# Attention and gated feed-forward on one core: the late heads' softmax weights transposed by VectorE and DMAs, their value products in float32 in two column streams

## The chip, the core and the metric

The program runs on one NeuronCore of a Trainium2 chip. The metric is the device time of one execution in microseconds (us); less is better. A core has a matrix engine (TensorE, called PE in the profile, its weight loads PEld), VectorE (DVE), ScalarE (ACT), GpSimd (POOL) and SyncE (SP), which here only issues DMAs. The engines run side by side, each through its own list of instructions in order, and wait for one another at semaphores.

## What is computed

Causal block attention for 8 batches and 8 heads (576 positions, head size 64, blocks of 64), and a feed-forward layer behind it, with 4608 tokens, width 512 and inner width 2048:

```python
scores = scale * np.matmul(q, k.transpose(0, 1, 3, 2))
mask = block_i >= block_j                       # blocks of 64 positions
scores = np.where(mask, scores, -1000000000.0)
scores = scores - np.max(scores, axis=-1, keepdims=True)
attn = np.exp(scores)
attn = attn / (np.sum(attn, axis=-1, keepdims=True) + 1e-09)
x = np.matmul(attn, v)                          # then heads side by side: 4608 x 512
h = x @ w_in
g = h * (1.0 / (1.0 + np.exp(-1.702 * h)))
out = g @ w_out
```

q, k and v are float32, and the two weight matrices arrive as float64.

## The kernel before, in words

**Two strands on one matrix engine.** The 64 heads are taken one after the other (loop at L568, one step a head). The feed-forward layer is a generator, `moe()` (L475), that is advanced between the parts of a head by `advance` (L543) until a quota of work for that point of the loop (`TILES_BY`, L35) is reached. It works on 12 tiles of 384 tokens. For each tile it goes over 16 chunks of the inner width; a chunk is 12 matmuls into the tile `hp` (L507) and, one chunk later, 9 matmuls into the three tiles `acc` (L479). In the steps of the late heads three chunks lie in a step, in six half portions: 36 matmuls `hp` and 27 matmuls `acc`. All matmuls keep the order in which the program writes them (`mm`, L92, and `tr`, L95).

**Chunks of queries.** The 576 queries of a head are cut into five chunks, i = 0 to 4, of 64, 128, 128, 128 and 128 rows; chunk i looks at 64 x (2i+1) keys. A step of the loop computes the scores of head n (`score`, L291, six parts S0 to S5; S4 and S5 are the two halves of chunk 4), and the value product of head n-1.

**What a score part does.** Two matmuls write the scores into a PSUM bank; DVE adds the mask, scales, and takes the row's extreme value (L313, into the tile `e` of the chunk); ACT takes the exponential and the row sum (L321); DVE turns the sums into reciprocals (L330, L333); the chunk is multiplied by them (L340 to L344, on the engine that `SCALE_ON` names).

**Early and late heads.** The first 17 heads (`EARLY`) and the other 47 differ. A late head loads q and k in strips (`load`, L194: four DMAs L214, two copies L218), turns them with a DVE transpose of 32x32 blocks (L244, L248) and splits them into a high and a low part (L245 to L250). For the value product the weights must stand with the keys on the partitions. `fill` (L368) does this before the change for all heads: PE transposes 128x128 blocks of `e` against an identity (L95, 15 a head, in four fills F1 to F4), and ACT copies the bank to `ph` (L386, L389). For a late head DVE also writes the rest into `pl` (L390) and mends the diagonal blocks (L396); the values are split in the same way into `vs` (L253, L254), with a copy `vd` made by two DMAs (L257). The value product `av` (L401), in two parts A and B, then is 14 matmuls of the format float32r (high and low parts against both halves of `vs`), and ACT and DVE add the two halves into `xr` (L430, L431). For an early head `av` is plain float32 against `vn`, and one float32 matmul stands in the profile as two records.

**The order of a step** is written out in `ORDER` (L28), one row for each phase; a blank there is where `moe()` is advanced. The late row before is `S0+F2 S1+F3 F4 S2 A S3 S4 F1+S5 B`.

Of the kernel before, what the change touches and what calls it, by code (L numbers as in the profile page):

```python
# [15 lines left out]
PSUM = bass.MemoryType.PSUM  # L16


EARLY = 17


SCALE_ON = ("APPPD", "DDPPP", "DDDDD")

GROUPS = (2, 3, 4)

ORDER = (  # L28
# [3 lines left out]
)  # L32

WEIGHTS_BY = ((0, 0), (9, 30), (15, 64))
TILES_BY = ((8.8, 0), (17, 1), (65, -2))  # L35
# [3 lines left out]
def attention_moe_kernel(  # L39
# [9 lines left out]
    nc = tc.nc  # L49
# [65 lines left out]
    for i in range(NCH):  # L115
# [2 lines left out]
        if i == 0:  # L118
            nc.gpsimd.memset(e[BLK:P, 0:BLK], 0.0)
        es.append(e)  # L120
    vr = sp.tile([P, NCH, D], F32, name="vr")
    nc.gpsimd.memset(vr[BLK:P, NCH - 1, :], 0.0)

    def width(i):
        return BLK * (2 * i + 1)
# [23 lines left out]

    def weight_piece(j, roomy):  # L150
        src, hi, lo = pieces[j]
        m = d2.tile([P, 2, WC], U32, tag=f"pl{1 + j % 2}", name="wm", bufs=1)
        halves = []
        for a in range(2):
            if roomy:
                w = xr[:, 2 * (j % 2) + a : 2 * (j % 2) + a + 1, S : S + 2 * WC].bitcast(U32)
            else:
                w = d2.tile([P, 1, 2 * WC], U32, tag="osb", name="wst", bufs=3)
            d = nc.sync.dma_start(out=w, in_=src[:, a : a + 1])
# [34 lines left out]
    def load(n):  # L194
        b, h = divmod(n, H)
        raw[n] = []
        for src in (q[b, h], k[b, h]):
            if early(n):

                t = d2.tile([P, NCH, 2, D], F32, tag="hl", name="qkr", bufs=3)  # L200
                parts = [
                    (t[:, 0:QC], src[0 : QC * P].rearrange("(p c) d -> p c d", c=QC).unsqueeze(2).to_broadcast([P, QC, 2, D])),
                    (t[0:BLK, QC], src[QC * P : S].unsqueeze(1).to_broadcast([BLK, 2, D])),
                ]
                queue = nc.scalar if n == 0 and len(raw[n]) else nc.sync
                for o, i in parts:
                    d = queue.dma_start(out=o, in_=i)
                    if n < 2:
                        tc.keep_in_program_order(d)
            else:  # L210

                t = d2.tile([P, S // 32, 32], F32, tag="hl", name="qkd", bufs=3)
                for c in range(0, D, 32):
                    nc.sync.dma_start(  # L214
                        out=t[c : c + 32],
                        in_=src[:, c : c + 32].rearrange("(c p) d -> p c d", p=32),
                    )
                nc.sync.dma_start(out=t[D:P], in_=t[0:D])  # L218
            raw[n].append(t)
        if not early(n):  # L220
            load_v(n, vr)

    def load_v(n, t):
        b, h = divmod(n, H)
        nc.sync.dma_start(
            out=t[:, 0:QC, :], in_=v[b, h, 0 : QC * P].rearrange("(c p) d -> p c d", p=P)
        )

        for r in (0,) if early(n) else (0, BLK):
            nc.sync.dma_start(out=t[r : r + BLK, QC, :], in_=v[b, h, QC * P : S])  # L230

    qk, vs, vd = {}, {}, {}

    def prep(n):
        qk1 = d2.tile([P, 2, S], F32R, tag="qk1", name="qk1")
# [12 lines left out]
        nc.vector.transpose(out=tmp, in_=kr.rearrange("p c d -> p (c d)"))  # L248
        nc.scalar.copy(out=k1, in_=tmp)
        subtract(nc.vector, k1[D:P], tmp[D:P], f(k1[D:P]))  # L250

        vs[n] = d2.tile([P, NCH, 2, D], F32R, tag="vs", name="vs")
        nc.scalar.copy(out=vs[n][:, :, 0, :], in_=vr)  # L253
        subtract(nc.vector, vs[n][:, :, 1, :], vr, f(vs[n][:, :, 0, :]))  # L254
        vd[n] = d2.tile([P, 2, D], F32R, tag="vd", name="vd")
        for r in (0, BLK):
            nc.sync.dma_start(out=f(vd[n][r : r + BLK]), in_=f(vs[n][0:BLK, 2]))  # L257

    def turn(n, which):
        qs, ks, qk1, q2 = qk[n]  # L260
# [30 lines left out]
    def score(n, ci):  # L291
# [42 lines left out]
        for ii in range(c0, i + 1):  # L334
# [7 lines left out]
                nc.vector.tensor_scalar(out=x, in0=x, scalar1=sc, scalar2=None, op0=ALU.mult)  # L342
# [10 lines left out]
    DIAG = ((2, 256), (4, 512))  # L353

    def blocks(j, q0, nq):
        res = []
# [11 lines left out]
    def fill(n, fi):  # L368


        pad, parts = FILLS[fi]
        tot = sum(p[2] for p in parts)
        bk = bank()
        tp = bk[:, pad : pad + tot]
        todo = []
        off = pad
        for j, q0, nq in parts:
            todo += [(j, off, *blk) for blk in blocks(j, q0, nq)]
            off += nq
# [3 lines left out]
        hi = d2.tile([P, tot], F32 if early(n) else F32R, tag=f"ph{fi}", name="ph", bufs=1)  # L383
        lo = None
        if early(n):
            nc.scalar.copy(out=hi, in_=tp[:, 0:tot])  # L386
        else:
            lo = d2.tile([P, tot], F32R, tag=f"pl{fi}", name="pl", bufs=1)
            nc.scalar.copy(out=hi, in_=tp[:, 0:tot])  # L389
            nc.vector.tensor_tensor(out=lo, in0=tp[:, 0:tot], in1=f(hi), op=ALU.subtract)  # L390
        off = 0
        for j, q0, nq in parts:
            c = slice(off, off + nq)
            pt[n, j, q0] = (hi[:, c], lo[:, c] if lo is not None else None)
            if not early(n) and (j, q0) in DIAG:
                nc.vector.tensor_tensor(  # L396
                    out=hi[BLK:P, c], in0=tp[BLK:P, c], in1=f(hi[BLK:P, c]), op=ALU.subtract
                )
            off += nq

    def av(n, parts, q0, nq):  # L401
# [2 lines left out]
        o = bank()  # L404
        r = (h % 2) * D
        c0 = (b % 2) * S + q0
        x = xr[r : r + D, h // 2, c0 : c0 + nq]

        todo = []
        for j, qs0, nn in parts:  # L410
            hi, lo = pt.pop((n, j, qs0))
            if early(n):
                kk = P if j < QC else BLK
                todo.append((vs[n][0:kk, j], hi[0:kk], qs0, nn))
            elif (j, qs0) in DIAG:
                vv = vs[n][:, j] if j == QC else vd[n]
                todo.insert(1, (vv.rearrange("p a d -> p (a d)"), hi, qs0, nn))
            else:
                vv = vs[n][:, j].rearrange("p a d -> p (a d)")
                todo[1:1] = [(vv, x, qs0, nn) for x in (hi, lo)]  # L420
        for cnt, (vv, w, qs0, nn) in enumerate(todo):
            mm(
                out=o[0 : vv.shape[1], qs0 - q0 : qs0 - q0 + nn], lhsT=vv, rhs=w,
                start=cnt == 0, stop=cnt == len(todo) - 1,
            )
        if early(n):
            (nc.scalar.copy if q0 else nc.vector.tensor_copy)(out=x, in_=o[0:D, 0:nq])  # L427
        else:

            nc.scalar.copy(out=x, in_=o[D - r : P - r, 0:nq])  # L430
            nc.vector.tensor_tensor(out=x, in0=o[r : r + D, 0:nq], in1=x, op=ALU.add)  # L431


    FILLS = [(0, PA[0:1]), (0, PB[0:1] + PA[1:3]), (0, PB[1:3]), (BLK, PB[3:5])]
# [1 line left out]
    def step(n):  # L436
# [4 lines left out]
        def on(c, fn, *a):  # L441
            return (lambda: fn(*a)) if c else None

        items = dict(
            F2=on(prev, fill, n - 1, 1), F3=on(prev, fill, n - 1, 2), F4=on(prev, fill, n - 1, 3),
            F1=on(now, fill, n, 0), A=on(prev, av, n - 1, PA, 0, SA), B=on(prev, av, n - 1, PB, SA, SB),
            Q=on(trn, turn, n + 1, 0), K=on(trn, turn, n + 1, 1), R=on(trn, turn, n + 1, 2),
        )
        for ci in range(6):
            items[f"S{ci}"] = on(now, score, n, ci)  # L450
        return [[items[y] for y in x.split("+")] for x in ORDER[phase(n)].split()]


    done = {"split": 0}
# [113 lines left out]
    for n in range(NHEAD + 1):  # L568
        if n + 1 < NHEAD:
            prep(n + 1)  # L570
        if n + 2 < NHEAD and not early(n + 1):
            load(n + 2)
        if n < NHEAD and early(n):
            vs[n] = d2.tile([P, NCH, D], F32, tag="vs", name="vn")
            load_v(n, vs[n])
        items = step(n)
        for sl, it in enumerate(items):
            for fn in it:
# [39 lines left out]
```

## Time and profile before

| | before |
|---|---|
| median of 3 runs | 1218.6 us (1217.72 to 1220.04) |
| profiled execution, its own time | 1218.16 us |
| its span, first to last instruction | 1216.4 us |
| instructions | 20880 |
| mean granted PE clock | 0.994 |
| DMA traffic | 78.62 MB |

The profile is of one execution. Its page gives each engine's busy time, the span in 40 slices, the chain of work that ended last, and groups of like instructions: line, engine, operation, output and input by the program's names, the count, and then the busy time, the mean of one in ns, and the idle time before them. The views used beside the page are the timeline (start, length, engine, line, with equal neighbours merged as x2, x3), the chain of waits in a window, and all instructions of one line with their shortest, median and longest length. Matmuls overlap: a record's length holds a drain that the next one covers, so that what one costs is the distance to the next start.

### The profile page before, as it was taken

To read this page: it belongs to the slowest core of one execution; us is meant where nothing else is said; L and a number is where in the kernel's file an instruction comes from. 1 tells how busy PE (TensorE), PEld (TensorE's weight loads), DVE (VectorE), ACT (ScalarE), POOL (GpSimd) and SP (SyncE) were. 2 spreads that over 40 slices of the span, in tenths; PEclk is the share of its full clock that TensorE was granted. 3 is DMA by queue.
4 is the path that set the end of the run, shared out by engine and by line. 5 is a ranking of instruction groups with operands and counts; after the bars stand their busy time and mean duration, and the time that the engine had idled before them with its cause. 6 is when DMAs were issued, how large, how long until landed. Compare 5 with 4: busy or idle time off the path is not lost.

```text
span 1216.4 us, 20880 instructions
## 1 busy us (share of the span) xinstructions
PE 1188.4 (98%) x6860; PEld 1063.9 (87%) x6860; DVE 872.0 (72%) x2460; ACT 706.7 (58%) x1773; POOL 367.6 (30%) x496
## 2 busy tenths in 40 slices
PE   6899999999999999999999999999999999999998
PEld 5667887789999999999999999999999999999997
DVE  6997788777887888778888787878788788611111
ACT  6886666655665565656665665565575566432322
POOL 3554454421321312321322232232132231232321
PEclk8999999999999999999999999999999999999999
DMA  8653444422222231232132232222232231000000
GB/s 201 162 152 94 118 117 119 108 42 51 50 70 44 55 76 40 48 81 50 38 76 55 44 70 50 51 70 45 53 76 43 46 77 30 4 26 1 27 1 26
DMA packets 223772, 78.62 MB, mean 65 GB/s; under 512 B 198832, under 2 KB 204848, under 8 KB 223664
## 3 DMA queue, kind: packets, MB, share of 16 engines
q1 hardware_dynamic: 222480, 77.00, 27.0%
q8 instruction: 54, 0.88, 0.3%
q14 instruction: 54, 0.44, 0.1%
q10 hardware_dynamic: 1184, 0.30, 0.1%
HBM read 50.87 MB, written 9.44 MB: 50 GB/s over the span
## 4 chain that ended last, share of the span: by engine, by line
PE 87%; DVE 7%; ACT 2%; issue 2%; DMA 1%; POOL 1%; POOLq 0%; SPq 0%; DVEq 0%; ACTq 0%
PE hp L92 32%; PE acc L92 32%; PE bank L92 15%; PE bank L95 8%; DVE e L313 1%; DVE wm L171 1%; DVE wm L176 1%; ACT e L321 1%; DVE sm L330 1%; DVE wm L167 1%; DVE e L342 1%; DVE qk L286 1%; DMA wst<-in_moe_w_out_dram 0%; DMA qkr<-in_q_dram 0%; DVE xr L427 0%
## 5 line engine op out<-in xcount | busy, mean ns | idle before, releaser
L81 POOL TENSOR_TENSOR gl<-g,gh 128x384 fp32r<-128x384 f32 x192 | 197.2, 1027 | 599.5 <-ACT gh L522 521.7
L321 ACT ACTIVATE e<-e,mx 64x64 f32<-64x64 f32 (+4 forms) x320 | 180.0, 563 | 214.8 <-DVE mx L313 213.8
L92 PE MATMUL hp<-xh,wih 128*128 128x384 f32 x768 | 268.0, 349 | 2.4 <-ACT wih L180 1.9
L92 PE MATMUL hp<-xl,wih 128*128 128x384 f32 x768 | 259.6, 338 | 1.2 <-POOL sm L297 1.2
L92 PE MATMUL hp<-xh,wil 128*128 128x384 f32 x768 | 259.0, 337 | 0.9 <-POOL wil L81 0.9
L92 PE MATMUL acc<-woh,gh 128*128 128x512 f32 x576 | 237.0, 412 | 0.5 <-ACT woh L180 0.5
L92 PE MATMUL acc<-wol,gh 128*128 128x512 f32 x576 | 227.2, 395 | 0.6 <-POOL wol L81 0.6
L92 PE MATMUL acc<-woh,gl 128*128 128x512 f32 x576 | 226.7, 394 | 0.5 <-POOL gl L81 0.5
L518 DVE SCALAR_TENSOR_TENSOR g<-g,hp 128x384 f32<-128x384 f32 x192 | 105.3, 548 | 129.4 <-ACT g L517 128.3
L313 DVE CUSTOM_DVE_ANT_0 e<-bank,mask 64x64 f32<-64x64 f32 (+4 forms) x320 | 132.9, 420 | 69.3 <-PE bank L92 65.6
L517 ACT ACTIVATE g<-hp 128x384 f32<-128x384 f32 x192 | 93.9, 489 | 119.2 <-PE hp L92 115.9
L95 PE MATMUL bank<-ident,e 128*128 128x128 f32 x960 | 153.9, 280 | 8.1 <-DVE e L342 5.6
L92 PEld LDWEIGHTS hp<-xh,wih 128*128 128x128 f32 x768 | 144.6, 188 | 11.5 <-ACT wih L180 2.1
L92 PEld LDWEIGHTS hp<-xh,wil 128*128 128x128 f32 x768 | 144.9, 189 | 9.6 <-POOL wil L81 1.2
L92 PEld LDWEIGHTS hp<-xl,wih 128*128 128x128 f32 x768 | 144.3, 188 | 1.6 <-POOL sm L297 1.6
L390 DVE TENSOR_TENSOR pl<-bank,ph 128x512 fp32r<-128x512 f32 (+2 forms) x188 | 102.4, 562 | 56.7 <-ACT ph L389 56.6
L342 DVE TENSOR_SCALAR e<-e,sm 64x64 f32<-64x64 f32 (+2 forms) x260 | 137.2, 557 | 4.9
L92 PEld LDWEIGHTS acc<-wol,gh 128*128 128x128 f32 x576 | 108.3, 188 | 26.2 <-POOL wol L81 1.1
L95 PEld LDWEIGHTS bank<-ident,e 128*128 128x128 f32 x960 | 112.1, 142 | 21.1 <-DVE e L342 8.0
L522 ACT CAST gh<-g 128x384 fp32r<-128x384 f32 x192 | 97.6, 508 | 52.9 <-DVE g L518 52.2
L92 PE MATMUL bank<-qk 128*128 128x320 f32 (+4 forms) x384 | 118.3, 308 | 2.7 <-DVE qk L286 1.8
L92 PEld LDWEIGHTS acc<-woh,gh 128*128 128x128 f32 x576 | 108.7, 189 | 11.0 <-ACT woh L180 0.7
(68 smaller groups left out, 1845.4 us busy)
## 6 DMA issues: line engine op xcount, KB each, us to landing
qkd<-qkd SPq DMA_DIRECT2D x94, 144.0 KB, 2.3
out_dram<-osb SPq DMA_DIRECT2D x36, 256.0 KB, 2.1
qkd<-in_q_dram SPq DMA_DIRECT2D x94, 72.0 KB, 2.4
qkd<-in_k_dram SPq DMA_DIRECT2D x94, 72.0 KB, 2.2
vr<-in_v_dram SPq DMA_DIRECT2D x47, 128.0 KB, 2.4
wst<-in_moe_w_out_dram SPq DMA_DIRECT2D x18, 256.0 KB, 3.2
qkr<-in_q_dram SPq DMA_DIRECT2D x17, 256.0 KB, 3.4
xr<-in_moe_w_in_dram SPq DMA_DIRECT2D x16, 256.0 KB, 3.1
```

The source lines that it names most:

```text
L81: eng.tensor_tensor(out=out, in0=in0, in1=in1, op=ALU.subtract)
L92: return tc.keep_in_program_order(nc.tensor.matmul(**kw))
L95: return tc.keep_in_program_order(nc.tensor.transpose(**kw))
L167: nc.vector.tensor_scalar(out=m, in0=m, scalar1=3, scalar2=None, op0=ALU.logical_shift_left)
L171: nc.vector.scalar_tensor_tensor(out=y, in0=w[..., 1], scalar=0x80000000, in1=y, op0=ALU.bitwise_and, op1=ALU.bitwise_or,)
L313: nc.vector.tensor_tensor_reduce(out=e[0:m, lo:hi], in0=s[0:m, 0 : hi - lo], in1=mk, op0=ALU.add, op1=ALU.min, scale=-0.125, scalar=3e38 i ...
L321: nc.scalar.activation(out=e[0:m, 0:w], in_=e[0:m, 0:w], func=AF.Exp, scale=-1.0, bias=mx[0:m, i : i + 1], accum_out=sm[0:m, i : i + 1],)
L342: nc.vector.tensor_scalar(out=x, in0=x, scalar1=sc, scalar2=None, op0=ALU.mult)
L390: nc.vector.tensor_tensor(out=lo, in0=tp[:, 0:tot], in1=f(hi), op=ALU.subtract)
L517: nc.scalar.activation(out=g, in_=hp[:, 0:tt], func=AF.Tanh, scale=1.702)
L518: nc.vector.scalar_tensor_tensor(out=g, in0=g, scalar=1.0, in1=hp[:, 0:tt], op0=ALU.add, op1=ALU.mult)
L522: nc.scalar.copy(out=gh, in_=g)
```

## The change

For early heads only buffers change: `fill` copies into slices of one tile `tw`, the values lie in the two tiles `v0` and `v1`, and the weight conversion uses `pw` as its scratch. For a late head:

- `fill`, `av`, the split of the values and the two DMAs of `vd` go. The fills, A and B are gone from the order.
- After a chunk is scaled, DVE transposes its 32x32 blocks into the tile `tw` (L355 of the changed kernel, chunks 1 to 4; L360, the 64x64 diagonal piece of each chunk). This turns each block in place and leaves it on the partitions of its queries.
- When chunk 4 is done, 16 DMAs on SP (L367) carry the blocks of each pair (block of keys, block of queries) to the partitions of their keys, in the tile `pw`. Each moves 32 partitions, one run of 1280 to 1792 bytes on each. There is one tile `tw` and one tile `pw`, used by every late head.
- `av_late`, item V, is 15 float32 matmuls against the unsplit values. Each has 64 columns of weights: those of chunks 4, 1 and 0 write PSUM partitions 0 to 63, those of chunks 3 and 2 partitions 64 to 127, and the two lists are merged by their position. 832 columns are streamed on one side and 768 on the other. ACT copies the result to `xr` in three pieces.
- The late row of the order is `S0+S1 S2 S3 S4 V S5`, and the step between the phases has a row of its own. V of head n-1 thus stands in step n, behind the fourth of six half portions of the feed-forward layer.
- Of a late head's five scalings, chunk 1's goes from DVE to POOL and chunk 3's from DVE to ACT; POOL's copies of L346 go.

```diff
-SCALE_ON = ("APPPD", "DDPPP", "DDDDD")
+SCALE_ON = ("APPPD", "DDPPP", "DPDAD")
...
-    "S0+F2 S1+F3 F4 S2 A S3 S4 F1+S5 B",
+    "S0+S1 S2 S3 S4 V S5",
...
+    NS = 14
+    SLOT = (None, 0, 1, 3, 6)
+    tw = sp.tile([P, 4 * NS * 32], F32, name="tw")
+    pw = sp.tile([P, 4 * NS * 32], F32, name="pw")
+    twv, pwv = [x.rearrange("p (b s c) -> p b s c", b=4, s=NS) for x in (tw, pw)]
...
-            if not early(n) and ii in (2, 4):
-                nc.gpsimd.tensor_copy(out=es[ii][BLK:P, we : we + BLK], in_=es[ii][BLK:P, we - BLK : we])
+            if early(n):
+                continue
+            if ii:
+                nc.vector.transpose(
+                    out=twv[:, :, SLOT[ii] : SLOT[ii] + ii, :].rearrange("p b j c -> p j b c"),
+                    in_=es[ii][:, 0 : ii * P],
+                )
+            r = slice(BLK, P) if ii else slice(0, BLK)
+            nc.vector.transpose(
+                out=twv[r, 0:2, 9 + max(ii, 1), :], in_=es[ii][r, ii * P : ii * P + BLK]
+            )
+        if not early(n) and i == NCH - 1:
+            for kb in range(4):
+                for qb in range(4):
+                    ns = 10 if kb > 1 else 14 if qb > 1 else 11
+                    nc.sync.dma_start(
+                        out=pwv[kb * 32 : kb * 32 + 32, qb, 0:ns, :],
+                        in_=twv[qb * 32 : qb * 32 + 32, kb, 0:ns, :],
+                    )
...
+    SIDES = (((4, 192), (1, 64), (0, 0)), ((3, 128), (2, 0)))
+
+    def av_late(n):
...
+        for side, chunks in zip((0, D), SIDES):
+            for i, c in chunks:
+                t = [(c, P, j, pwv[:, :, SLOT[i] + j, :]) for j in range(i)]
+                a, w = (2, c + BLK) if i else (0, c)
+                t.append((w, BLK, i, pwv[:, a : a + 2, 9 + max(i, 1), :]))
+                for w, nn, j, rhs in t:
+                    todo.append((sum(y[1] for y in todo if y[2] == side), nn, side, w, j, rhs))
+        todo.sort(key=lambda y: y[0])
...
+        for x, (pos, nn, side, w, j, rhs) in enumerate(todo):
+            mm(
+                out=o[side : side + D, w : w + nn].rearrange("d (a c) -> d a c", c=32),
+                lhsT=v2[n % 2][:, j], rhs=rhs, start=pos == 0, stop=x == ends[side],
+            )
```

SP's list before, one late head: `qkd` are strips of q and k, `vr` the values, `vd` the copy of a piece of the split values.

```order
L218 DMA qkd<-qkd 64x576
L214 DMA qkd<-in_q_dram 32x18x32 x2
L218 DMA qkd<-qkd 64x576
L214 DMA qkd<-in_k_dram 32x18x32 x2
L257 DMA vd<-vs 64x128 x2
L225 DMA vr<-in_v_dram 128x4x64
L230 DMA vr<-in_v_dram 64x64 x2
```

SP's list after, one late head: the 16 DMAs from `tw` to `pw` and then the loads of the next heads.

```order
L367 DMA pw<-tw 32x352 x2
L367 DMA pw<-tw 32x448 x2
L367 DMA pw<-tw 32x352 x2
L367 DMA pw<-tw 32x448 x2
L367 DMA pw<-tw 32x320 x8
L235 DMA qkd<-qkd 64x576
L231 DMA qkd<-in_k_dram 32x18x32 x2
L241 DMA v_90<-in_v_dram 128x4x64
L244 DMA v_90<-in_v_dram 64x64
L231 DMA qkd<-in_q_dram 32x18x32
L235 DMA qkd<-qkd 64x576
L231 DMA qkd<-in_q_dram 32x18x32
```

SP issues 24 DMAs a late head where it issued 11, and the 16 stand in one row without anything between them.

PE's list before, the larger part of a late head's value product (B), between two groups of `hp`:

```order
L92 MATMUL bank<-ph,vs 128x256
L92 MATMUL bank<-ph,vs 128x64
L92 MATMUL bank<-ph,vs 128x192
L92 MATMUL bank<-pl,vs 128x192
L92 MATMUL bank<-ph,vs 128x256
L92 MATMUL bank<-pl,vs 128x256
L92 MATMUL bank<-ph,vs 128x256
L92 MATMUL bank<-pl,vs 128x256 x2
```

PE's list after, the whole value product (V), with the last matmul of the group of `hp` ahead of it and the first of the group of `acc` behind it:

```order
L96 MATMUL hp<-xl,wih 128x384
L96 MATMUL bank<-pw,v_92 64x128 x7
L96 MATMUL bank<-pw,v_92 64x64
L96 MATMUL bank<-pw,v_92 64x128
L96 MATMUL bank<-pw,v_92 64x64
L96 MATMUL bank<-pw,v_92 64x128 x2
L96 MATMUL bank<-pw,v_92 64x64 x3
L96 MATMUL acc_5947<-woh,gh 128x512
```

The rows of `ident,e`, 15 a head before, are gone. The first matmul of V waits for all 16 DMAs of its head.

DVE's list between the two halves of chunk 4 before, with what each row waits for (`e_86` is chunk 3, `e_88` chunk 4):

```order
L313 ISA e_88,mx<-bank,mask 128x256 [waits PE_49]
L313 ISA mx 128x1
L330 TENSOR_SCALAR sm<-sm 128x1 [waits Activation_49]
L518 SCALAR_TENSOR_TENSOR g<-g,hp 128x384 [waits Activation_49]
L333 RECIPROCAL sm<-sm 128x1 [waits DVE_49]
L342 TENSOR_SCALAR e_86<-e_86,sm 128x448 [waits DVE_49]
L313 ISA e_88,mx<-bank,mask,mx 128x320 [waits PE_49]
```

The same place after (`e_82` is chunk 1, `e_84` chunk 2):

```order
L360 STREAM_TRANSPOSE tw<-e_86 64x2x32 [waits Activation_49]
L546 SCALAR_TENSOR_TENSOR g<-g,hp 128x384 [waits Activation_49]
L355 STREAM_TRANSPOSE tw<-e_82 128x4x32 [waits DMAHW4_49,DMAHW5_49,DMAHW3_49,DMAHW6_49,DMAHW2_49,DMAHW7_49,DMAHW1_49,DMAHW0_49]
L355 STREAM_TRANSPOSE tw<-e_84 128x2x4x32
L355 STREAM_TRANSPOSE tw<-e_86 128x3x4x32
L258 STREAM_TRANSPOSE tmp<-qkd 128x576 [waits DMAHW0_49]
L320 ISA e_88,mx<-bank,mask,mx 128x320 [waits DVE_49,PE_49]
```

The transposes of chunks 1 to 3 wait until the DMAs of the head before have read `tw`. Chunk 4's two transposes stand after its scaling and S0's reduction of the next step, and the 16 DMAs wait for them.

More of the change, by code (lines that the diff above doesn't have):

```diff
@@ L227, in load_v @@
         )
-        for r in (0,) if early(n) else (0, BLK):
-            nc.sync.dma_start(out=t[r : r + BLK, QC, :], in_=v[b, h, QC * P : S])
-    qk, vs, vd = {}, {}, {}
+        nc.sync.dma_start(out=t[0:BLK, QC, :], in_=v[b, h, QC * P : S])
+    qk = {}
     def prep(n):
@@ L382, in fill @@
             tr(out=bk[:, c : c + P], in_=es[i][:, j * P : (j + 1) * P], identity=ident)
[L383 to L390, printed above, removed]
+        o = sum(sum(p[2] for p in x[1]) for x in FILLS[:fi])
+        hi = tw[:, o : o + tot]
+        nc.scalar.copy(out=hi, in_=tp)
         off = 0
         for j, q0, nq in parts:
[L393 to L398, printed above, removed]
+            pt[n, j, q0] = hi[:, off : off + nq]
             off += nq
@@ L421, in av @@
-        for cnt, (vv, w, qs0, nn) in enumerate(todo):
-            mm(
-                out=o[0 : vv.shape[1], qs0 - q0 : qs0 - q0 + nn], lhsT=vv, rhs=w,
-                start=cnt == 0, stop=cnt == len(todo) - 1,
-            )
[L426 to L431, printed above, removed]
+        for cnt, (j, qs0, nn) in enumerate(parts):
+            kk = P if j < QC else BLK
+            mm(
+                out=o[0:D, qs0 - q0 : qs0 - q0 + nn], lhsT=v2[n % 2][0:kk, j], rhs=pt.pop((n, j, qs0))[0:kk],
+                start=cnt == 0, stop=cnt == len(parts) - 1,
+            )
@@ L444, in step @@
         items = dict(
+            V=on(prev and not early(n - 1), av_late, n - 1),
             F2=on(prev, fill, n - 1, 1), F3=on(prev, fill, n - 1, 2), F4=on(prev, fill, n - 1, 3),
@@ L572, in attention_moe_kernel @@
             load(n + 2)
[L573 to L575 removed]
+        if n < NHEAD:
+            load_v(n)
+        if n == EARLY:
+            nc.gpsimd.memset(pwv[BLK:P, :, 10:NS, :], 0.0)
         items = step(n)
```

50 lines of the change are left out of this document (24 added, 26 removed).

## The prediction

> **What bounds the kernel now.** I read the page's busy times first, then the chain of waits inside one late head, then one stage by engine.
>
> ```profile
> span 1216.4 us, 20880 instructions
> PE 1188.4 (98%) x6860; PEld 1063.9 (87%) x6860; DVE 872.0 (72%) x2460; ACT 706.7 (58%) x1773; POOL 367.6 (30%) x496
> 400.00:600.00 200.00, 200.00 (x1187) 184.81 (x1185) 161.50 (x443) 118.75 (x297) 49.41 (x76) 1.00 0.26 56
> ```
>
> The last row is a window in the middle of the late heads: PE has no idle time, DVE is busy 161.50 of 200 us, ACT 118.75, and the granted clock is 1.00. In the chain of waits between 400 and 418 us every piece is PE's own (start, length, tile and line, records):
>
> ```profile
> by line: PE hp L92 38.0%; PE acc L92 34.6%; PE bank L92 17.8%; PE bank L95 11.2%
> ...
> 400.18 0.33 PE bank L95 x3
> ...
> 401.86 1.39 PE acc L92 x6
> 403.25 0.63 PE bank L92 x5
> 403.88 0.69 PE acc L92 x3
> ...
> 408.73 0.33 PE bank L95 x3
> 409.06 0.30 PE bank L92 x2
> ...
> 411.13 1.06 PE bank L92 x9
> ...
> 413.33 0.60 PE bank L95 x5
> ...
> 415.51 0.44 PE bank L95 x4
> ...
> 417.71 0.33 PE bank L95 x3
> ```
>
> The same fill returns at 417.71, 17.53 us after 400.18: that is the period of a late head, and PE fills it without a gap. So before the change the end is set by the sum of PE's work, and a us taken off PE in each of the 47 late heads is 47 us, as long as nothing else takes PE's place.
>
> **What PE loses and gains.** The fills (L95: 0.33, 0.60, 0.44 and 0.33) are 1.70 us of a period and the two value products (0.63 and 1.06) 1.69 us. Both go: 3.39 us a head, and 14.14 us stay. V is new. Its price is read at the float32 value product of an early head, which has the same 64 columns of weights; the timeline of PE and PEld:
>
> ```profile
> 111.81 0.39 PE L92 MATMUL acc<-woh,gl 128*128 128x512 f32 x1
> 112.05 0.40 PE L92 MATMUL acc<-wol,gh 128*128 128x512 f32 x1
> 112.37 0.65 PE L92 MATMUL bank<-ph,vn 128*64 128x256 f32 x2
> 112.37 0.86 PE L92 MATMUL bank<-ph,vn 128*64 128x256 f32 x3
> 112.37 1.49 PEld L92 LDWEIGHTS bank<-ph,vn 128*64 128x64 f32 x8 [0.37 <-issue]
> 114.39 0.50 PE L92 MATMUL acc<-woh,gh 128*128 128x512 f32 x1
> 114.73 0.39 PE L92 MATMUL acc<-woh,gl 128*128 128x512 f32 x1
> ```
>
> Two answers end after two and after three records: a third of 256 columns adds 0.21 us, 0.82 ns a column. A float32 matmul is two such records. V's longer stream, 832 columns, is 2 x 832 x 0.82 ns = 1.37 us if the shorter one runs beside it; both one after the other are 2 x 1600 x 0.82 = 2.62 us. Around it the array changes from 128 to 64 columns: the first record starts 0.32 us behind an `acc` where the `acc` before it took 0.24, and behind the block the first `acc` takes 0.34. That is 0.09 and 0.10 us, and about as much again for the first load and the gap at the end; I count 0.35 us. No trace of before has two streams at once; I take them side by side, because they write different partitions and have different columns of weights. V then is 1.75 us (3.0 in sequence), and PE's own sum is 14.14 + 1.75 = 15.89 us a head.
>
> Side by side is also what the Trainium skill says ("TensorEngine Tiling (Array Packing)", Key Properties: tiles operate independently); no run here shows it yet.
>
> **The new wait.** V waits for its head's 16 DMAs; these wait for DVE's transposes of chunk 4; these for S5. From S5 to V, PE has the rest of its sum to do, 15.89 less V, an `acc` group (0.69 + 1.39 = 2.08) and S5 (0.30): 11.76 us. If DVE, ACT and the DMAs take longer, PE stands at V, and everything in its list behind V stands with it. The chain up to the DMAs, on PE, ACT and DVE, in the present kernel:
>
> ```profile
> 812.35 0.31 PE L92 MATMUL bank<-qk,q 128*128 128x320 f32 x1
> 812.70 0.55 DVE L313 CUSTOM_DVE_ANT_0 e<-bank,mask,mx 128x320 f32<-128x320 f32 x1 [0.23 <-PE bank L92]
> 813.30 0.78 ACT L321 ACTIVATE e<-e,mx 128x576 f32<-128x576 f32 x1
> 814.25 0.15 DVE L330 TENSOR_SCALAR sm<-sm 128x1 f32<-128x1 f32 x1
> 814.38 0.78 DVE L248 STREAM_TRANSPOSE tmp<-qkd 128x576 f32<-128x576 f32 x1
> 815.08 0.12 DVE L333 RECIPROCAL sm<-sm 128x1 f32<-128x1 f32 x1
> 815.24 0.52 DVE L342 TENSOR_SCALAR e<-e,sm 128x576 f32<-128x576 f32 x1
> 817.51 0.20 DVE L313 CUSTOM_DVE_ANT_0 e<-bank,mask 64x64 f32<-64x64 f32 x1
> ```
>
> From S5's second matmul at 812.35 to the end of the scaling at 815.76 are 3.41 us. The transpose between (814.38 to 815.08) stands ahead of S5 in the new list: 2.71 us. Behind the scaling come S0's reduction, 0.20, and the transpose of chunk 4, 512 columns. The nearest row:
>
> ```profile
> L244 DVE STREAM_TRANSPOSE tmp<-qkd 128x576 f32<-128x576 f32 x47 | 36.0, 765 | 0.5 <-DVE sm L330 0.4
> L390 DVE TENSOR_TENSOR pl<-bank,ph 128x512 fp32r<-128x512 f32 (+2 forms) x188 | 102.4, 562 | 56.7 <-ACT ph L389 56.6
> L431 DVE TENSOR_TENSOR xr<-bank,xr 64x320 f32<-64x320 f32 x47 | 22.8, 485 | 2.0 <-ACT xr L430 1.3
> ```
>
> 512/576 of 765 ns are 0.68 us. With 0.05 to reach SP the first DMA starts 2.71 + 0.20 + 0.68 + 0.05 = 3.64 us behind S5's second matmul.
>
> **The 16 DMAs** are the disputed cost. SP's rows, by line (shortest, median, longest in ns) and in the timeline:
>
> ```profile
> L214 SPq DMA_DIRECT2D qkd<-in_k_dram x94: 311/489/1622, 211.6 to 1008.5; - x94
> L257 SPq DMA_DIRECT2D vd<-vs x94: 467/536/772, 220.2 to 1045.0; - x94
> 18.25 0.33 SPq L159 DMA_DIRECT2D xr<-in_moe_w_out_dram  x1
> 18.64 0.42 SPq L159 DMA_DIRECT2D wst<-in_moe_w_out_dram  x1
> 796.80 1.11 SPq L257 DMA_DIRECT2D vd<-vs  x2
> 797.96 0.58 SPq L225 DMA_DIRECT2D vr<-in_v_dram  x1
> 798.58 1.15 SPq L230 DMA_DIRECT2D vr<-in_v_dram  x2
> 799.77 1.12 SPq L214 DMA_DIRECT2D qkd<-in_k_dram  x2
> vd<-vs SPq DMA_DIRECT2D x94, 32.0 KB, 1.8
> qkd<-qkd SPq DMA_DIRECT2D x94, 144.0 KB, 2.3
> ```
>
> A DMA holds SP for 0.3 to 0.6 us, longer when another stands right ahead, and 0.05 us lie between two (18.25 + 0.33 to 18.64). The trains differ: 128 partitions with one run each (L159) 0.42 + 0.05 = 0.47 us a DMA; 32 partitions with 18 runs each (L214) 0.49 + 0.05 = 0.54; 64 partitions (L257, L230) about 0.60 (796.80 to 798.58 are three DMAs, 0.59 each), and up to 0.64. The new DMAs have 32 partitions and one run on each. The only rows with 32 partitions are the cheapest when alone (0.31), and their train carries 18 runs a partition; fewer runs should cost no more, so I take 0.47, between the ends 0.43 and 0.64. Landing: 32 KB take 1.8 us, 144 KB 2.3; for at most 56 KB I take 1.9.
>
> The loop from V to the next V then is V 1.75 + `acc` 2.08 + S5's first matmul 0.15 + 3.64 + 15 x 0.47 = 7.05 + 1.9 = 16.57 us. It is longer than PE's sum, 15.89: PE waits 0.68 us at every V, and a late head takes 16.57 us, not 17.53. In general the loop is 9.52 us + 15 times the distance of two DMAs; it meets PE's sum at 0.425 us and the present period at 0.534 us.
>
> **The other edits.** DVE loses L390 (102.4 / 47 = 2.18 us a head), L431 (its two parts 0.9) and more; it gains 1280 columns of transposes, 1.33 ns each, 1.70 us, and five pieces of 64 columns at about 0.2, as S0's reduction takes. So its share stays near 0.8 and the transposes are hidden, but for chunk 4's 0.68. DVE's transposes of chunks 1 to 3 wait for the same DMAs as V and have V, `acc` and S5 as cover (4.0 us for 1.02 + 0.77 of L258); behind them only S5's reduction is queued. ACT loses four copies and gains three smaller ones and a scaling; POOL swaps two copies for one scaling. SP issues 24 DMAs a head, 11.3 to 14.4 us, inside the period. The early heads' edits cost nothing: same copies, other buffers.
>
> **The sum.** 47 x (17.53 - 16.57) = 45 us. In the last step no scores stand ahead of V and PE waits about 1 us more. The profiled execution took 1218.16 us by its own time, 0.4 below the median of the runs and inside their spread, so no correction is made: 1218.2 - 44 = 1174 us. This likeliest case by itself goes from 1145 (0.43 us a DMA) to 1210 (0.52).
>
> **The rivals.**
> - *The queue becomes the bound* (slower; chance 0.29). At the price of the 64-partition rows, 0.64, the loop is 19.12 us, 1.59 more than now: 1218 + 75 = 1293 us; at 0.59 it is 1258. It decides from 0.534 on. For it: `vd` too goes from SBUF to SBUF with one run a partition. Against it: the 32-partition rows are cheaper. With it PE would stand 2 to 3 us at each V.
> - *The queue is hidden* (faster; 0.08). Below 0.425 PE's sum remains: 47 x 1.64 = 77 us, 1141 us.
> - *The two streams run in sequence* (slower; 0.07). V is 3.0 us; with my price for the DMAs the loop is 17.82: 1232 us.
> - *The loads stand out* (slower; 0.02). The eight loads at 112.37 lie inside their block, so a load goes on beside the running matmul. If alternating sides undid that, each of 30 records would expose half of the 0.10 us that the 128-column load showed: 1.5 us, loop 18.07, 1243 us. The Trainium skill ("TensorE: Matmul & The Clock Gate", Part 3) says that a load overlaps a running matmul only where the row groups differ, and both sides use all rows; the eight loads, all on the same rows, do not agree.
> - *No difference* (0.04): a distance of about 0.53.
>
> **How the numbers follow.** A measurement of this kernel tells about 0.2% from no change, 2.4 us. Faster: 0.50 + 0.08 = 0.58. Same: 0.04. Slower: 0.29 + 0.07 + 0.02 = 0.38. The range reaches from 1140, with the hidden queue, to 1258, a distance of 0.59 us; what lies above, about 0.18, is left out.
>
> **What would show it.** In the new profile: the distance of two L367 rows on SP (0.47); their landing (1.9); PE's idle time ahead of V, by the release of a `pw` DMA (0.7 us, 47 times); the period (16.6); V's 30 records in 1.4 us, in pairs. Wrong would be: V over 2.5 us, a distance above 0.53, or a larger wait that another engine ends, DVE's `g` above all.

## The result and the profile after

The changed kernel takes 1393.59 us (median of 4 runs, 1390.01 to 1402.86), the kernel before 1218.16 us beside it: a ratio of 1.145, 95% interval 1.139 to 1.151. It is 175 us slower; the prediction had 45 us faster, and even its slow rival had 1293.

The page of the changed kernel: the span, the engines' busy shares, the granted clock in 40 slices, and the chain that ended last by engine and by line.

```profile
span 1388.8 us, 21590 instructions
PE 1196.5 (86%) x6907; PEld 1045.0 (75%) x6907; DVE 767.1 (55%) x2366; ACT 647.7 (47%) x1632; POOL 371.4 (27%) x451
...
PEclk9999999998988999899999999998998999899999
...
PE 37%; SPq 25%; DVE 19%; DMA 7%; issue 6%; ACT 5%; POOL 0%; DVEq 0%; POOLq 0%; ACTq 0%
SPq L367 25%; PE acc L96 15%; PE bank L96 13%; PE hp L96 7%; DMA pw<-tw 6%; DVE e L320 3%; ACT e L328 2%; DVE e L349 2%; DVE tw L355 2%; DVE q L85 2%; DVE tmp L262 2%; ACT qk L259 1%; DVE g L546 1%; DVE qk L85 1%; PE bank L99 1%
```

Before, PE was 98% busy and every piece of the chain inside a late head was its own. Now PE is 86% busy, and the largest line of the chain is L367, SP issuing the 16 DMAs. The waits of the late heads say where PE stands (total us, times, longest):

```profile
PE bank L96 <- DMA pw<-tw: 148.6, 47, 5.2
...
DVE tw L355 <- DMA pw<-tw: 90.3, 46, 4.0
...
DVE g L546 <- ACT g L545: 65.9, 47, 3.7
```

47 times, once a head, PE stands 148.6 / 47 = 3.16 us ahead of V for the last DMA. The place is the predicted one, the size is not (0.68 us). One head, V to V, from two windows of the timeline; the rows of DVE show the chain behind S5:

```profile
802.74 2.93 PE L96 MATMUL bank<-pw,v 128*64 128x128 f32 x30 [3.25 <-DMA pw<-tw]
...
805.60 0.50 PE L96 MATMUL acc<-woh,gh 128*128 128x512 f32 x1
...
807.94 0.31 PE L96 MATMUL bank<-qk,q 128*128 128x320 f32 x1
808.28 0.55 DVE L320 CUSTOM_DVE_ANT_0 e<-bank,mask,mx 128x320 f32<-128x320 f32 x1 [3.77 <-PE bank L96]
...
810.34 0.52 DVE L349 TENSOR_SCALAR e<-e,sm 128x576 f32<-128x576 f32 x1
...
810.92 0.70 DVE L355 STREAM_TRANSPOSE tw<-e 128x512 f32<-128x512 f32 x1
...
811.72 10.04 SPq L367 DMA_DIRECT2D pw<-tw  x16
...
823.54 0.66 PE L96 MATMUL bank<-pw,v 128*64 128x128 f32 x8 [2.91 <-DMA pw<-tw]
```

Each start less the one before is a term of the predicted loop. The right column is the mean over the 46 distances from V to V, read in the same way from the trace:

| term | predicted, us | this head | mean of 46 |
|---|---|---|---|
| V | 1.75 | 2.86 | 2.64 |
| `acc` and S5's first matmul | 2.23 | 2.34 | 2.61 |
| S5's second matmul to the first DMA | 3.64 | 3.78 | 4.10 |
| first to last DMA | 7.05 | 9.45 | 9.65 |
| last DMA to V | 1.90 | 2.37 | 2.09 |
| loop | 16.57 | 20.80 | 21.09 |

The 16 DMAs last 10.04 us with 0.59 for the last: (10.04 - 0.59) / 15 = 0.63 us apart. 47 x (21.09 - 17.53) = 167 us of the 175 are this loop; the rest lies ahead of the first of these V's and behind the last.

V itself has two prices (2.5 us and more for 37 of the 47, under 1.8 for 8). Windows of three V's: from and to, their length, busy time (records) of PE, PEld, DVE, ACT and POOL, PE's granted clock, the DMA share and GB/s:

```profile
781.68:784.61 2.93, 2.93 (x30) 2.82 (x30) 1.81 (x4) 0.00 (x0) 0.00 (x0) 0.50 0.72 141
...
802.74:805.60 2.86, 2.86 (x31) 2.79 (x31) 1.77 (x4) 0.00 (x0) 0.00 (x0) 0.53 0.72 140
823.54:825.09 1.55, 1.55 (x30) 1.49 (x30) 1.03 (x3) 0.00 (x0) 0.00 (x0) 1.00 0.36 61
```

The same 30 records take 1.55 us at a clock of 1.00 and 2.93 at 0.50. The `acc` group behind V pays too where the clock stays low: in the slowest heads its term is 3.2 to 3.7 us instead of 2.34. So two things had to be tested: what sets 0.63 us, and whether the wait itself makes V dear.

### The profile page after: what moved, and what is told of

It is laid out like the page before. It is cut to its first block, busy times and chain, and to the rows that moved or that the text cites. A ratio compares the mean times of both kernels' runs of the same rounds, so it can differ in the third digit from the quotient of the medians.

```text
span 1388.8 us, 21590 instructions
## 1 busy us (share of the span) xinstructions
PE 1196.5 (86%) x6907; PEld 1045.0 (75%) x6907; DVE 767.1 (55%) x2366; ACT 647.7 (47%) x1632; POOL 371.4 (27%) x451
## 4 chain that ended last, share of the span: by engine, by line
PE 37%; SPq 25%; DVE 19%; DMA 7%; issue 6%; ACT 5%; POOL 0%; DVEq 0%; POOLq 0%; ACTq 0%
SPq L367 25%; PE acc L96 15%; PE bank L96 13%; PE hp L96 7%; DMA pw<-tw 6%; DVE e L320 3%; ACT e L328 2%; DVE e L349 2%; DVE tw L355 2%; DVE q L85 2%; DVE tmp L262 2%; ACT qk L259 1%; DVE g L546 1%; DVE qk L85 1%; PE bank L99 1%
## 5 line engine op out<-in xcount | busy, mean ns | idle before, releaser
L85 POOL TENSOR_TENSOR gl<-g,gh 128x384 fp32r<-128x384 f32 x192 | 196.6, 1024 | 452.1 <-ACT gh L550 408.2
L96 PE MATMUL bank<-pw,v 128*64 128x128 f32 (+1 forms) x1410 | 127.8, 361 | 148.6 <-DMA pw<-tw 148.6
L96 PE MATMUL acc<-woh,gh 128*128 128x512 f32 x576 | 245.0, 425 | 1.2 <-ACT woh L197 1.2
L96 PEld LDWEIGHTS bank<-pw,v 128*64 128x64 f32 x1410 | 120.8, 207 | 162.4 <-issue 127.6
L96 PE MATMUL acc<-woh,gl 128*128 128x512 f32 x576 | 233.2, 405 | 0.5 <-POOL gl L85 0.5
L96 PE MATMUL acc<-wol,gh 128*128 128x512 f32 x576 | 232.1, 403 | 0.6 <-POOL wol L85 0.6
L546 DVE SCALAR_TENSOR_TENSOR g<-g,hp 128x384 f32<-128x384 f32 x192 | 105.1, 548 | 196.6 <-ACT g L545 196.2
L320 DVE CUSTOM_DVE_ANT_0 e<-bank,mask,mx 128x320 f32<-128x320 f32 x64 | 35.1, 548 | 193.7 <-PE bank L96 193.2
L455 ACT COPY xr<-bank 64x192 f32<-64x192 f32 x141 | 44.0, 312 | 197.7 <-PE bank L96 196.5
L355 DVE STREAM_TRANSPOSE tw<-e 128x128 f32<-128x128 f32 (+3 forms) x188 | 84.6, 487 | 90.4 <-DMA pw<-tw 90.3
L96 PEld LDWEIGHTS acc<-woh,gh 128*128 128x128 f32 x576 | 114.5, 199 | 24.4 <-ACT woh L197 1.4
L96 PEld LDWEIGHTS acc<-woh,gl 128*128 128x128 f32 x576 | 114.3, 198 | 18.6 <-POOL gl L85 0.9
```

What stands on the lines that cost most here:

```text
L85: eng.tensor_tensor(out=out, in0=in0, in1=in1, op=ALU.subtract)
L96: return tc.keep_in_program_order(nc.tensor.matmul(**kw))
L320: nc.vector.tensor_tensor_reduce(out=e[0:m, lo:hi], in0=s[0:m, 0 : hi - lo], in1=mk, op0=ALU.add, op1=ALU.min, scale=-0.125, scalar=3e38 i ...
L355: nc.vector.transpose(out=twv[:, :, SLOT[ii] : SLOT[ii] + ii, :].rearrange("p b j c -> p j b c"), in_=es[ii][:, 0 : ii * P],)
L455: nc.scalar.copy(out=xr[r : r + D, h // 2, c0 + q0 : c0 + q0 + nq], in_=o[side : side + D, w : w + nq])
L546: nc.vector.scalar_tensor_tensor(out=g, in0=g, scalar=1.0, in1=hp[:, 0:tt], op0=ALU.add, op1=ALU.mult)
```

## The experiments

The theory after the result: the loop V, S5, DVE, 16 DMAs on SP, V sets the period; its queue term was priced too low, and the wait halves PE's clock for V. The rivals: V is slow by itself, as two streams that do not run side by side or with loads that stand out; DVE or ACT set the period.

**Half of the DMAs left out.**

```
-            for kb in range(4):
+            for kb in range(2):
```

> Of each late head's 16 DMAs the eight with kb = 2 and 3 are left out (the value products then read zeros in half of their rows, all instructions of TensorE stay). My theory: the loop from V over S5, DVE and the DMAs on SP back to V sets the period of a late head, 21.1 us, and 15 distances of two DMAs at 0.63 us are its largest piece. Eight distances less, 5.1 us, and V at 1.55 instead of 2.64 us, since TensorE's wait ahead of it goes, leave a loop of 14.9 us, below TensorE's own sum of some 15.7 us: 47 x (17.53 - 15.7) = 86 us below the kernel before, about 1132 us. Rival, V itself (two streams that TensorE works off slowly, 2.9 us whatever comes ahead): the sum would be 17.0 us, 1195 us, and V's records keep their 213 ns a pair. Rival, DVE or ACT set the period: no more than a few us of 1394 go.

Measured: 1190.9 us. The wait at V is gone, and PE's other wait is what is left (272 to 1250 us, the late heads):

```profile
PE hp L96 <- DVE g L546: 21.2, 40, 1.9
PE hp L96 <- DVE sm L337: 2.0, 2, 1.0
...
PE bank L96 <- DMA pw<-tw: 0.3, 1, 0.3
```

203 us go with eight DMAs, so the train of DMAs is the bound and neither V nor DVE is. The expected 1132 was too low: most heads take 16.57 us and the mean is 16.80, not 15.7. Of the difference of 1.1 us, 21.2 / 47 = 0.45 us a head are the wait for `g`; the rest was not followed up.

**Work put into the wait.**

```
         ends = {y[2]: x for x, y in enumerate(todo)}
+        for x in range(10):
+            mm(out=o, lhsT=woh[:, 0, 0:P], rhs=woh[:, 0, :], start=True, stop=True)
```

> Ten float32r matmuls of 128x512 that nobody reads stand ahead of V in every late head, 2.3 us of extra work for TensorE in each. My theory: V costs 2.93 us in most heads and 1.55 in some because TensorE stood idle for about 3 us ahead of it and its granted clock was halved; with the idle time filled, V takes 1.55 us in every head, the loop is 1.09 us shorter on average, and 47 x 1.09 = 51 us go: about 1342 us, although work was added. Rival, V is slow because of its loads or of contention for SBUF or PSUM: V stays at 2.9 us and the time at 1394 us. Rival, TensorE's sum is the bound: 47 x 2.3 = 108 us more, 1502 us.

Measured: 1340.7 us, 53 us less with 2.47 us more work a head. The window of one V (columns as above):

```profile
656.40:657.95 1.55, 1.55 (x30) 1.49 (x30) 1.08 (x3) 0.00 (x0) 0.00 (x0) 1.00 0.51 85
```

The ten extra matmuls and V behind them, in the timeline:

```profile
653.09 2.47 PE L96 MATMUL bank<-woh 128*128 128x512 f32 x10
656.40 0.84 PE L96 MATMUL bank<-pw,v 128*64 128x128 f32 x11 [0.84 <-DMA pw<-tw]
```

V takes 1.55 to 1.58 us in 45 of the 47 heads, the DMAs are as far apart as before, and the loop is 1.10 us shorter (19.99 in place of 21.09), about 1.0 of it V's. That the idle time makes V dear is shown; the loads and the streams are not the cause.

**The same bytes over 128 partitions.**

```
-                        out=pwv[kb * 32 : kb * 32 + 32, qb, 0:ns, :],
-                        in_=twv[qb * 32 : qb * 32 + 32, kb, 0:ns, :],
+                nc.sync.dma_start(out=pw[:, c], in_=tw[:, c])
```

Here `c` is a run of three or four slots of one `qb`; the 16 of them cover the tile.

> The 16 DMAs of a late head move the same bytes straight across, all 128 partitions with 384 or 512 bytes each, instead of 32 partitions with 1280 to 1792 bytes each (the blocks do not change their partitions, so the products are of other data; nothing else changes). This is the price that the prediction took from the 128-partition weight loads. If the shape sets it: 0.47 us or less a DMA, 15 x 0.16 = 2.4 us a head less than with 0.633, and TensorE's shorter wait may give back up to 1.1 us more at V: 1230 to 1281 us. If a transfer from SBUF to SBUF costs 0.6 us in a train whatever its shape: no more than 0.03 us a DMA changes, about 1375 to 1394 us.

Measured: 1204.8 us. The train and the V that waits for it, in the timeline:

```profile
812.84 10.31 SPq L367 DMA_DIRECT2D pw<-tw  x16
...
820.94 0.66 PE L96 MATMUL bank<-pw,v 128*64 128x128 f32 x8
...
821.93 0.62 PE L96 MATMUL bank<-pw,v 128*64 128x128 f32 x6 [0.33 <-DMA pw<-tw]
```

The distance is (10.31 - 0.60) / 15 = 0.65 us: the number of partitions does not set it, and the 128-partition rows were cheap for another reason. The time fell all the same, by a side effect that the expectation missed. V starts at 820.94, while the train still runs to 823.15: a DMA across all partitions completes whole slots, so V's first products need only some of the DMAs. In the changed kernel each product reads slots that all 16 fill, and V can start only behind the last.

**The same blocks, read from DRAM.**

```
-                        in_=twv[qb * 32 : qb * 32 + 32, kb, 0:ns, :],
+                        in_=flat[r : r + 32, 0 : ns * 32],
```

> The 16 DMAs of a late head write the same 32-partition blocks, but read them from q in DRAM instead of tw in SBUF (so the value products are of other data, and the DMAs no longer wait for the transposes). It measures the disputed price by itself: if reading from SBUF makes a DMA dear in a train, the distance falls from 0.633 to the 0.38 to 0.47 us of the weight loads; if any train of 16 costs as much, it stays at 0.60 to 0.64. Either way the DMAs start right behind V, the loop over them is 1.55 + 15 x 0.63 + 2.1 = 13.1 us at most, and TensorE's sum bounds: 1175 to 1195 us.

Measured: 1265.1 us. The train of 16 in one head, in the timeline; the row of its line (shortest, median, longest in ns); and the same rows of the changed kernel for L367 and for the output's stores:

```profile
846.80 7.31 SPq L369 DMA_DIRECT2D pw<-in_q_dram  x16
```

```profile
L369 SPq DMA_DIRECT2D pw<-in_q_dram x752: 310/419/2084, 21.7 to 1111.9; - x188
```

```profile
L367 SPq DMA_DIRECT2D pw<-tw x752: 507/589/1783, 259.7 to 1240.4; - x188
...
L518 SPq DMA_DIRECT2D out_dram<-osb x36: 332/394/583, 237.0 to 1385.8; - x36
```

The distance is (7.31 - 0.42) / 15 = 0.46 us, with destination, shape, number and queue unchanged. So, for these blocks, 0.46 is the price of a train that reads DRAM, and 0.63 that of one from SBUF to SBUF. A store from SBUF to DRAM has a median of 0.39 (alone or a few in a row), and no `pw<-tw` takes less than 0.51, so the source alone does not do it. A source in DRAM is no promise either: one load of `v`, 64 partitions of 256 bytes, has a median of 0.51 in the changed kernel.

```profile
L244 SPq DMA_DIRECT2D v<-in_v_dram x64: 489/514/1565, 5.2 to 1203.8; - x64
```

What makes these dear was not tested. The time of the run was not the expected 1175 to 1195: a head took 18.47 us, and in 400 to 1200 PE waited 74.8 us for `g`. Why `g` was that late was not followed up.

**Two queues.**

```
-                    nc.sync.dma_start(
+                    (nc.scalar if qb % 2 else nc.sync).dma_start(
```

> The DMAs with odd qb are issued by ACT instead of SP, eight on each queue. My theory: the distance of 0.633 us is the price of one engine's issue; two engines issue side by side, the last DMA starts 7 x 0.63 = 4.4 us behind the first instead of 9.5, V falls to 1.55 us, and the loop is 15.0 us, below TensorE's sum. ACT is held for about 5 us a head, which can delay the tanh that the hidden layer waits for: 1132 us without such a wait, up to 1200 with 1.5 us of it a head. Rival, the price lies behind the issuing engines, in the transfers themselves: the landing grows by what the issue saves, and the time stays near 1390 us.

Measured: 1436.9 us, 1.179 of the kernel before (1.175 to 1.182), slower than with one queue. ACT's rows and the two trains, in the timeline:

```profile
838.62 0.19 ACT L328 ACTIVATION_READ_ACCUMULATOR e<-e,mx 128x1 f32 x1
838.85 5.33 SPq L367 DMA_DIRECT2D pw<-tw  x8
838.85 5.04 ACTq L367 DMA_DIRECT2D pw<-tw  x8
...
843.93 0.51 ACT L550 CAST gh<-g 128x384 fp32r<-128x384 f32 x1 [5.12 <-DMA pw<-tw]
```

PE's largest wait in that kernel's late heads (272 to 1250 us):

```profile
PE hp L96 <- DVE g L546: 170.4, 47, 6.4
```

The price is one of the issuing engine, as the theory says: both queues issue side by side, 0.63 us apart on ACT and 0.68 on SP in these trains, and the wait at V is gone. But ACT is held for 5.1 us, with the next exponentials and casts behind the DMAs in its list; DVE waits for these, `g` stands behind them on DVE, and PE waits 170.4 / 47 = 3.6 us a head for `g`. The price was moved onto an engine that the loop needs too; it was expected to cost at most 1.5 us a head.

**The two sides in sequence.**

```
-        todo.sort(key=lambda y: y[0])
+        todo.sort(key=lambda y: y[2])
```

> V's matmuls are the same, but all of the first column side come ahead of all of the second. If the sides run side by side in the kernel as it is, which its records say (two start 0.04 us apart, the next pair 0.21 us on), V doubles: 30 records of 0.107 us and 0.21 us at half clock are 2.9 us where TensorE's clock was kept and 5.3 where it was halved; on average 2.2 us more a head, about 1500 us. If the two streams run one after the other anyway (the prediction's rival), nothing changes: V 2.6 us, 1394 us.

Measured: 1427.7 us, 34 more. Two V's of it:

```profile
840.89:843.59 2.70, 2.70 (x30) 2.64 (x30) 0.88 (x3) 0.00 (x0) 0.00 (x0) 1.00 0.41 84
1208.50:1213.60 5.10, 5.05 (x30) 5.04 (x30) 1.10 (x3) 0.00 (x0) 0.00 (x0) 0.50 0.48 93
```

2.70 us in place of 1.55 at the full clock, 5.1 in place of 2.93 at the half: interleaved, the streams do run side by side. V's mean is 3.76 us, 1.1 more than before, not 2.2: 19 of the 47 V's ran at the full clock, and only 8 at the half clock to their end.

**V behind S5, and behind the next head's DMAs.**

```
-    "S0+S1 S2 S3 S4 V S5",
+    "S0+S1 S2 S3 S4 S5 V",
```

> V of the head before stands behind S5 instead of ahead of it, so S5 no longer waits for V. My theory: the loop then closes over DVE. Its transposes of chunks 0 to 2 of the next head write the same buffer, stand in DVE's list between S2's and S3's reductions and wait for the last DMA's landing, some 15.8 us behind S5 (4.1 + 9.65 + 2.1); from there to the next first DMA lie S3, S4 and S5 with their work on DVE and ACT and what TensorE does between them, 4 to 9 us: a loop of 20 to 25 us, no gain (1340 us and more), and the wait is named as a transpose on DVE that waits for a DMA of pw. Rival, the prediction's view that these transposes have cover: only TensorE's sum is left, 16.6 to 16.8 us as with eight DMAs, 1175 to 1195 us.

> As the run before, and all transposes of a head stand behind the scaling of chunk 4, so that nothing of the next head's scores is queued behind their wait. My theory: from the last landing, 15.8 us behind S5, only 2.7 us of transposes lead to the next first DMA, and these can start at S5 + 3 us of the next head at the earliest; the loop over the DMAs is 9.65 + 2.1 + 2.7 + 0.3 = 14.8 us and TensorE's sum with its waits for g, 16.6 to 16.8 us, is the bound: 1175 to 1195 us, faster than both kernels. Rival, SP or the DMAs are the bound by themselves (24 DMAs a head): SP's issues, 16 x 0.63 + 8 x 0.55 = 14.5 us, fit, but if the loads of q and k come late behind the train, 18 us and more, above 1240 us.

Measured: 1906.4 us (1.567 of before, 1.564 to 1.569) and 1885.2 us (1.549, 1.547 to 1.552). The first one's wait:

```profile
PE bank L96 <- DMA pw<-tw: 634.7, 46, 16.3
```

Neither answers what it was made for. S5's function also issues its head's transposes and DMAs, so a V that stands behind it in the program waits for the DMAs just started and reads the next head's weights. PE stands 634.7 / 46 = 13.8 us at each V: the whole loop without cover.

**V behind S5, ahead of its own head's transposes and DMAs.** S5 loses both; a new item T has them:

```
-    "S0+S1 S2 S3 S4 V S5",
+    "S0+S1 S2 S3 S4 S5 V+T",
```

> What the two runs before were meant to be: S5, then V of the head before, then the transposes of all five chunks and the 16 DMAs of the head's own (in the two runs before, these stood ahead of V in the program, so V waited for the DMAs just started and read the next head's weights; here V reads its own, nothing is left out). My theory: V and S5 no longer stand in one loop with the DMAs. From a last landing only the transposes, 2.7 us, and the issue lead to the next first DMA: 2.7 + 9.65 + 2.1 + 0.1 = 14.6 us; V has its data some 17.9 us behind its own S5 and stands 2.3 us behind the next one. What is left is TensorE's sum with its waits for g, 16.0 to 16.8 us a head: 1150 to 1190 us, faster than the kernel before, V at 1.55 us. Rival, SP: its loads of q, k and v stand behind the train and wait for buffers, and a load that waits holds the next train: 18 us and more, above 1240 us.

> As the run with it, but the transposes stay where they are in the changed kernel, behind the scaling of their chunks; only V and the DMAs are moved behind S5. My theory: DVE's transposes of chunks 0 to 2 stand ahead of S3's reduction and wait for the last landing of the head before, 15.8 us behind its S5; behind them come g, the reductions of S3, S4 and S5 and the scaling and transposes of chunk 4, 5 to 9 us until the next first DMA, so a loop of 17 to 21 us: 1200 to 1380 us, with DVE's wait for a DMA of pw in the trace. Rival, the transposes do not matter, V's place alone does: the same time as the run with it, within 10 us.

Measured: 1205.0 us with the transposes in T, 0.991 of the kernel before (0.990 to 0.993), and 1202.9 us with the transposes left in their place. PE's wait in the first, and SP's list in one of its long heads:

```profile
PE bank L96 <- DMA pw<-tw: 41.9, 27, 4.0
```

```profile
978.07 0.53 SPq L525 DMA_DIRECT2D out_dram<-osb  x1
978.70 0.66 SPq L235 DMA_DIRECT2D qkd<-qkd  x1
979.42 1.06 SPq L525 DMA_DIRECT2D out_dram<-osb  x2
980.59 10.21 SPq L369 DMA_DIRECT2D pw<-tw  x16
```

With all 16 DMAs at their 0.63 us the time falls by 189 us, because V and S5 are no longer between one train and the next. Both kernels lie about 1% below the one before, a gain under 2% that is clear of the noise in the first (the second ran once). Counted from S5 to S5, the shortest heads of the first take 15.96 us, TensorE's own sum; 8 of 45 take 18.9 to 21.5, and in long heads the wait at V comes back. The second run does not tell what it was made for: the transposes of chunks 1 to 3 did not stay in their place. The four large ones of a head stand in one row behind chunk 4's scaling (probably because their buffer is free only then):

```profile
956.66 1.69 DVE L355 STREAM_TRANSPOSE tw<-e 128x128 f32<-128x128 f32 x4
```

So whether their old place would close a loop over DVE was not tried.

**The output stored by ACT**, on top of the second of these:

```
-                    nc.sync.dma_start(out=out[r : r + P, :], in_=osb)
+                    nc.scalar.dma_start(out=out[r : r + P, :], in_=osb)
```

> As e10_turns_in_place, and the output tiles are stored by ACT's queue instead of SP's. In the run before, 9 or 10 of 47 heads took 18.7 to 20.7 us, one in five, as often as an output tile ends, the others 16 to 17 us; there SP's list holds a store of the output and a copy of q or k ahead of the first DMA of a train. My theory: these waits of SP make the train late, and TensorE stands some 3.5 us at V in those heads; without them every head takes 16.0 to 16.8 us, 47 x 16.5 against 47 x 16.94 = 20 us less or more: 1165 to 1185 us. Rival, the pause comes from the tile's other work on ACT and DVE (the casts of the next tile, the last copies of acc): the time stays at 1200 to 1205 us.

Measured: 1199.9 us, 0.985 of the kernel before (0.983 to 0.987), the lowest median of a kernel that does all the work. PE's wait at V:

```profile
PE bank L96 <- DMA pw<-tw: 39.3, 30, 3.1
```

Only 3 of the expected 20 us came, and the run before (1202.9) lies inside the spread of this kernel's own runs (1194.8 to 1203.0), so no gain of this edit is shown. From S5 to S5, 4 of 45 heads take over 18.5 us instead of 7, but 13 between 17 and 18.5 instead of 6, and the wait at V is 39 us where it was 35. What delays the train in these heads stays open.

## Why the prediction was wrong

*PE's sum* was right: 15.89 us a head predicted, 15.96 in the shortest heads once the train was out of the way. So was *side by side*: V 1.75 us predicted (1.37 + 0.35 is 1.72, rounded up), 1.55 measured at the full clock, and 2.70 in sequence where 3.0 was given. The Trainium skill's rule that tiles operate independently ("TensorEngine Tiling (Array Packing)", Key Properties) agrees with these two numbers.

*The place of the new wait* was right: V, 47 times, released by a `pw` DMA, inside the loop as it was written down.

*The step that failed* is the price of a DMA: "fewer runs should cost no more, so I take 0.47". It chose among the rows by partitions and runs a partition. The runs show that 128 partitions in place of 32 do not make it cheaper (0.65) and that a source in DRAM does (0.46 for the same blocks). What counted here was the one property named "for" the rival and then set aside, that `vd` goes from SBUF to SBUF. Its 0.59 to 0.64 was the nearest row; 0.63 was measured. The train is 2.6 of the 4.5 us by which the loop is longer. The argument that the 32-partition rows are the cheapest also rested on a misreading: the 0.49 behind L214's 0.54 is the median of DMAs that stand alone and of others in a row. The two at 799.77, which the prediction shows, start 0.63 us apart.

*The second step that failed* also spoiled the rival: V was priced at the full clock on every path. "With it PE would stand 2 to 3 us at each V", the rival says, and then it prices V at 1.75. Such a wait can halve the clock for what comes behind it: 0.9 us of the mean V, most of the 0.38 by which the `acc` term is longer, and 53 us in all by the run with the filled wait. It explains half of the distance from the rival's 1293 us to the measured time.

*The chain to the first DMA* was short by 0.46 us in the mean: 3.6 us, as predicted, where nothing else stands in it, 4.1 where DVE also splits q (L85, 0.75 us) ahead of the transposes, and 4.5 in early ones of the late heads. There the transpose of L262, taken to stand ahead of S5, takes 0.78 us ahead of the scaling, and `g` (L546) stands between the scaling and the transposes; these rows of the changed kernel's timeline are from such a head:

```profile
518.11 0.55 DVE L320 CUSTOM_DVE_ANT_0 e<-bank,mask,mx 128x320 f32<-128x320 f32 x1 [4.54 <-PE bank L96]
...
519.60 0.78 DVE L262 STREAM_TRANSPOSE tmp<-qkd 128x576 f32<-128x576 f32 x1
...
520.66 0.51 DVE L349 TENSOR_SCALAR e<-e,sm 128x576 f32<-128x576 f32 x1
521.09 0.54 DVE L546 SCALAR_TENSOR_TENSOR g<-g,hp 128x384 f32<-128x384 f32 x1
```

*The gain behind the queue* was also too large: with eight DMAs, and no wait at V, the kernel takes 1191 us where 1141 was given for a hidden queue. Of these 50 us PE's wait for `g` on DVE is 21; the rest stays open.

## What to carry to other kernels

Price a train of DMAs from a row with the same source and destination memory whose DMAs follow one another as yours will, not from a median that has lone ones in it, and count the train whole wherever one consumer needs all of it. When a wait of a few us ahead of TensorE is forecast, price what follows at both clocks. A consumer placed so that the next train does not depend on it can make a dear train harmless: the same 16 DMAs gave 1394 us in one place of V and 1203 in another.

## What the runs showed of the hardware

- The issue price on SP, per DMA in a train of 16: 0.63 us from SBUF to SBUF with 32 partitions, 0.65 with 128, 0.46 from DRAM to SBUF with 32. ACT issues eight at the same 0.63 beside SP, and its own instructions stand behind them for 5.1 us.
- The granted clock went from 1.00 to 0.50 for a V behind some 3 us of idle time. The length of the wait alone does not decide: 2.45 us were enough ahead of 358.80, 2.98 were not ahead of 492.61. In the clock's records of the changed kernel, every stretch of one clock between its changes is a whole number of windows of 3.41 us on one fixed grid. Between 300 and 1245 us the clock fell at the end of all 39 windows at 1.00 in which PE, by its records, stood idle for 1.91 us or more, and of none of the 190 with 1.89 or less; the other runs part at the same place, but for two falls at 1.78 in the run from DRAM. Two such windows, each with the next (columns as for V):

```profile
354.90:358.31 3.41, 1.45 (x9) 1.13 (x7) 1.16 (x4) 1.97 (x4) 0.69 (x2) 1.00 0.24 65
358.31:361.72 3.41, 2.92 (x30) 2.85 (x30) 1.10 (x3) 0.00 (x0) 0.83 (x1) 0.50 0.92 282
...
819.11:822.52 3.41, 1.52 (x9) 1.20 (x7) 1.22 (x5) 1.41 (x3) 0.85 (x2) 1.00 0.24 65
822.52:825.93 3.41, 2.39 (x34) 2.22 (x35) 1.10 (x3) 0.70 (x3) 0.90 (x1) 1.00 0.49 96
```

So whether a wait of 2 to 4 us costs depends on where it lies on the grid. The Trainium skill ("TensorE: Matmul & The Clock Gate", Part 1) gives an idle window of about 3.4 us that runs freely, so that the point varies. The trace agrees with the window and with the varying point, but not with a window that has to be idle throughout: 1.91 us of the 3.41 were enough.

- Two float32 column streams of 64 columns of weights each run side by side if their matmuls alternate (1.55 us against 2.70 in sequence). The longer stream's columns are 1.37 us of the 1.55, so 30 loads on alternating sides left at most 0.18 us exposed.
